# Two sequences in one tile, a second array shape and another load order in a pooled-attention and gated-convolution kernel

## The chip, the cores and the metric

The kernel runs on one core of one Trainium2 chip. The metric is the device time of one execution in microseconds (us), inputs and output in the chip's main memory. A core has five engines that run their own instruction streams: TensorE (PE in the profile, with weight loads as PEld), VectorE (DVE), ScalarE (ACT), GpSimd (POOL) and SyncE (SP). Here GpSimd does almost nothing but issue loads, and SP nothing but issue DMAs. The timed runs of the kernel before took 256.58, 256.73 and 257.45 us.

## The reference

Eight sequences of 576 rows, 8 heads of 64. Keys and values are averaged over groups of 8 rows (72 remain), attention is computed against these, and its result goes through a feed-forward block with a convolution of three taps along the sequence, one weight per channel, whose sigmoid gates the hidden layer.

```python
k_p = k.reshape(B, H, Sp, pool, D).mean(axis=3)          # pool = 8, Sp = 72
v_p = v.reshape(B, H, Sp, pool, D).mean(axis=3)
scores = scale * np.matmul(q, k_p.transpose(0, 1, 3, 2))
scores = scores - np.max(scores, axis=-1, keepdims=True)
attn = np.exp(scores)
attn = attn / (np.sum(attn, axis=-1, keepdims=True) + 1e-09)
x = np.matmul(attn, v_p)                                 # then [B, S, 8 * 64]
h = np.maximum(x @ w_in, 0.0)                            # w_in [512, 1024]
conv_out = sum of conv_w[k] * h shifted by k - 1 rows    # per channel
gate = 1.0 / (1.0 + np.exp(-conv_out))
out = (h * gate) @ w_out                                 # w_out [1024, 512]
```

## The kernel before

All matrix work is in bf16. The 576 rows of a sequence are ordered so that row 9p + c lies in column block c (9 blocks of 64). An attention tile is 128 rows by 8 heads: a sequence has four full tiles and one half tile. `groups = [[0], [1], [2, 3], [4, 5], [6, 7]]` (line 272) says which sequences share one: in a pair the two half tiles become one full tile, so a pair has 9 tiles, while sequences 0 and 1 have 5 each. The second sequence of a pair keeps its rows in another block order, and its convolution (`conv_runs`, line 683) is cut in 20 matmuls a block of channels in place of 16.

The steps of a sequence b are:

- `prep_k` (438) pools k by a matmul with the matrix pm, `prep_q` (484) transposes q on TensorE, `prep_v` (458, 462) adds v up on VectorE and spreads it into vm. The copies out of PSUM (449, 492) go to VectorE or ScalarE.
- Per tile: scores (517), the negative maximum (530), its addition (by TensorE, 550, in groups 0 and 1; by VectorE into sd, 542, later), the exponential into e (563), the transpose of e into eT (on TensorE with a copy, 575 and 589, or a DMA transpose issued by SP, 584, from group 3 on), values (600), division (613, 615) into x, and the transpose of x into xT (632 and 640 on TensorE, or a DMA transpose by SP, 624, for groups whose first sequence is 2 or more).
- The feed-forward part: w_in (645; for sequence 0 tile by tile, 666), the rectifier into hT (654, 676), a copy hX of hT with its two halves of 64 channels swapped (711), the convolution in four 64x64 quadrants (731), tanh (743), the gate and the product into gT (753, 754), w_out (761), the copy to osb (772), the store (783).

A step of the swap (`ffn_swap`, 711) is a copy by VectorE or ScalarE for sequences 0 to 3, and a DMA issued by SP for 4 to 7 (`SWAP_DVE = 4`). A swap serves two blocks of channels, so a sequence has four pairs of swaps.

The order of everything is the work of a planner, the class `Graph`. Each step is added with a key, an assumed duration on each engine that may do it, what must come before and which buffers it uses. `order` (91) keeps an assumed clock for each engine and takes the startable step of the smallest key; a step that two engines may do goes to the one with the smaller key or less work so far. The keys are sums of a slot per sequence and numbers of a table (`ATT`, `PREP_K`, `NUDGE` and so on). The result is one fixed program per engine. Each engine works through its own in order, and waits only for semaphores. Where TensorE has nothing to do early on, the planner puts in matmuls on a blank tile (432), which compute nothing that is used.

Loads go by GpSimd's queue (329 for q and k, 343 and 346 for v, 354 for w_in, 357 for w_out), with a cast from float32 to bf16; stores, transposes and swaps go by SP's queue.

Of the kernel before, what the change touches and what calls it, by code (L numbers as in the profile page):

```python
# [32 lines left out]
class Graph:  # L33
# [57 lines left out]
    def order(self):  # L91
# [5 lines left out]
        wire, mode, now, done = 0.0, None, 0.0, []  # L97
# [3 lines left out]
        spares = list(self.spares)  # L101
# [54 lines left out]

        while avail:
# [4 lines left out]
            for o in avail:  # L162
# [80 lines left out]
def kernel(  # L243
# [261 lines left out]
    def rows_of(g, t):  # L505
        return parts(g, t)[-1][1]
# [598 lines left out]
```

## Time and profile before

| | us |
|---|---|
| timed runs, median (lowest to highest) | 256.73 (256.58 to 257.45) |
| profiled execution, whole | 257.26 |
| profiled execution, span from first to last instruction | 255.2 |
| first full-speed slices of TensorE's clock | from about 24 |
| swaps on VectorE / ScalarE / by DMA | 14 / 18 / 32 instructions |

The profile has busy times per engine, groups of equal instructions (xcount, busy us, mean ns, idle time before them and what ended it), the chain of work that ended last, followed backwards from the end, timelines, and stretches of time with the busy time of each engine in them. Instructions that follow each other on an engine can overlap by some tens of nanoseconds, so that group times add up to a little more than the engine's. The table below is of groups and issues that the change touches.

```profile
L449 ACT CAST kT<-psum 64x288 bf16<-64x288 f32 x11 | 4.3, 393 | 2.4 <-PE psum L438 2.3
L589 DVE COPY eT<-psum 128x640 bf16<-128x640 bf16 x6 | 2.9, 485 | 1.5 <-PE psum L575 1.4
...
out_dram<-osb SPq DMA_DIRECT2D x72, 128.0 KB, 2.4
hX<-hT SPq DMA_DIRECT2D x32, 144.0 KB, 2.4
xT<-x SPq DMA_TRANSPOSE x27, 3.2
eT<-e SPq DMA_TRANSPOSE x18, 2.6
```

The last four rows are DMA issues: count, size, median time from issue to landing.

### The profile page before, as it was taken

What the parts mean: (1) busy time and instruction counts of PE and PEld (TensorE: products, weight loads), DVE (VectorE), ACT (ScalarE), POOL (GpSimd) and SP (SyncE); (2) the same over time, 40 slices, a digit from 0 to 9 for tenths busy, and PEclk for the clock granted to TensorE, in tenths of its full rate; (3) what the DMA queues carried; (4) which work ended last, traced back from release to release, by engine and by line L of the source; (5) the groups of instructions that cost most, each with busy time, mean ns of one, the idle gap of its engine ahead of it and who ended that gap; (6) DMA issues with size and microseconds to landing.
All of it is one profiled execution on the core that took longest, in us unless ns stands there. A gap on an engine that the chain in (4) does not pass through costs nothing.

```text
span 255.2 us, 7524 instructions
## 1 busy us (share of the span) xinstructions
PE 228.6 (90%) x3169; PEld 158.1 (62%) x3169; DVE 168.8 (66%) x363; ACT 164.8 (65%) x259; POOL 30.0 (12%) x50
## 2 busy tenths in 40 slices
PE   5758999989998899999999969879899889999992
PEld 1526888877776567567765536656565466676440
DVE  6557687799999998999568779411679711716200
ACT  2225547679899949986896455436688435758431
POOL 7753311302040004000001000000000000000000
PEclk9658999999999999999999999999999999999998
DMA  5999999999979558976408776668856859736356
GB/s 82 149 197 207 208 208 206 206 207 208 171 104 180 119 97 153 174 153 124 84 3 137 159 111 133 134 89 192 184 124 136 132 119 214 154 89 142 84 135 153
DMA packets 50682, 37.40 MB, mean 147 GB/s; under 512 B 29121, under 2 KB 43481, under 8 KB 50649
## 3 DMA queue, kind: packets, MB, share of 16 engines
q1 hardware_dynamic: 35176, 20.67, 40.7%
q0 software_dynamic: 15472, 16.26, 39.5%
q8 instruction: 24, 0.39, 0.6%
q14 instruction: 10, 0.07, 0.1%
HBM read 32.52 MB, written 9.44 MB: 164 GB/s over the span
## 4 chain that ended last, share of the span: by engine, by line
PE 49%; DVE 17%; DMA 14%; ACT 9%; SPq 4%; issue 3%; POOL 2%; ACTq 0%; POOLq 0%; DVEq 0%
PE psum L761 17%; PE psum L645 10%; PE psum L731 7%; DMA hX<-hT 6%; DMA qp<-in_q_dram 3%; DMA eT<-e 3%; DVE negm L530 3%; DVE x L615 3%; PE psum L666 3%; PE psum L600 3%; ACT hX L711 2%; PE psum L484 2%; PE psum L517 2%; ACT hT L654 2%; ACT e L563 2%
## 5 line engine op out<-in xcount | busy, mean ns | idle before, releaser
L761 PE MATMUL psum<-w_out_sb,gT 128*128 128x512 bf16 (+1 forms) x296 | 70.6, 379 | 0.7 <-DVE x L615 0.3
L645 PE MATMUL psum<-xT,w_in_sb 128*128 128x288 bf16 x448 | 59.2, 286 | 1.2 <-ACT xT L640 0.6
L645 PEld LDWEIGHTS <-w_in_sb 128*128 128x128 bf16 x448 | 42.5, 98 | 13.1 <-issue 0.8
L654 ACT ACTIVATE hT<-psum 128x576 bf16<-128x576 f32 x56 | 34.4, 649 | 18.1 <-PE psum L645 18.0
L743 ACT ACTIVATE tg<-psum 128x576 bf16<-128x576 f32 x64 | 38.0, 654 | 11.4 <-PE psum L731 6.7
L761 PEld LDWEIGHTS <-gT 128*128 128x128 bf16 (+1 forms) x296 | 27.1, 98 | 28.1 <-issue 1.0
L772 ACT COPY osb<-psum 128x512 f32<-128x512 f32 (+1 forms) x31 | 18.0, 583 | 24.4 <-PE psum L761 23.8
L731 PE MATMUL psum<-hX,dw 64*64 64x288 bf16 (+4 forms) x560 | 31.6, 249 | 2.4 <-DMA hX<-hT 2.4
L731 PEld LDWEIGHTS <-dw 64*64 64x64 bf16 x1120 | 25.4, 107 | 13.1 <-issue 11.6
L731 PE MATMUL psum<-hT,dw 64*64 64x288 bf16 (+4 forms) x560 | 31.8, 249 | 1.5 <-DVE x L615 0.5
L753 DVE TENSOR_SCALAR tg<-tg 128x576 bf16<-128x576 bf16 x64 | 19.7, 308 | 19.0 <-ACT tg L743 18.9
L530 DVE TENSOR_REDUCE negm<-psum 128x8 f32<-128x576 f32 (+2 forms) x37 | 26.9, 751 | 7.4 <-PE psum L517 7.0
L754 DVE TENSOR_TENSOR gT<-tg,hT 128x576 bf16<-128x576 bf16 x64 | 29.3, 458 | 2.2
L615 DVE TENSOR_TENSOR x<-psum,r 128x512 bf16<-128x512 f32 (+1 forms) x37 | 25.6, 691 | 1.5 <-DVE r L613 0.2
L600 PE MATMUL psum<-vm,eT 128*128 128x130 bf16 (+5 forms) x240 | 18.5, 222 | 7.0 <-DMA eT<-e 5.3
L613 DVE RECIPROCAL r<-psum 128x8 f32<-128x8 f32 (+1 forms) x37 | 7.4, 201 | 24.7 <-PE psum L600 24.5
L600 PEld LDWEIGHTS <-eT 128*128 128x128 bf16 (+1 forms) x240 | 14.2, 100 | 13.7 <-DMA eT<-e 8.3
L563 ACT ACTIVATE e<-sd 128x576 bf16<-128x576 f32 x27 | 18.0, 681 | 5.6 <-DVE sd L542 5.4
L711 ACT COPY hX<-hT 64x1152 bf16<-64x1152 bf16 x18 | 20.7, 1150 | 0.4
L542 DVE TENSOR_TENSOR sd<-psum,negm 128x576 f32<-128x576 f32 x27 | 19.6, 751 | 0.3
L438 PE MATMUL psum<-pm,kp 128*64 128x144 bf16 x288 | 13.6, 235 | 3.3 <-DMA kp<-in_k_dram 3.3
L492 ACT COPY qT<-psum 128x1152 bf16<-128x1152 bf16 (+2 forms) x13 | 12.2, 992 | 6.5 <-PE psum L484 6.5
(61 smaller groups left out, 221.0 us busy)
## 6 DMA issues: line engine op xcount, KB each, us to landing
out_dram<-osb SPq DMA_DIRECT2D x72, 128.0 KB, 2.4
hX<-hT SPq DMA_DIRECT2D x32, 144.0 KB, 2.4
v<-in_v_dram POOLq DMA_DIRECT2D x8, 512.0 KB, 9.9
kp<-in_k_dram POOLq DMA_DIRECT2D x7, 576.0 KB, 18.7
qp<-in_q_dram POOLq DMA_DIRECT2D x7, 576.0 KB, 12.9
w_in_sb<-in_moe_w_in_dram POOLq DMA_DIRECT2D x4, 256.0 KB, 9.5
w_out_sb<-in_moe_w_out_dram POOLq DMA_DIRECT2D x1, 1024.0 KB, 17.1
kp<-in_k_dram POOLq DMA_DIRECT2D x2, 288.0 KB, 5.3
```

The source lines that it names most:

```text
L530: nc.vector.tensor_reduce(out=a["m"][0:rows], in_=a["s"][0:rows, :, 0:2 * KW].rearrange("p a (h s) -> p a h s", s=Sp), axis=AX.X, op=OP.ma ...
L563: nc.scalar.activation(out=e[0:rows, 0:4 * KW].rearrange("p (a x) -> p a x", a=2), in_=a["d"][0:rows].rearrange("p a h s -> p a (h s)") if ...
L600: nc.tensor.matmul(out=a["o"][lo:hi, h // 4, (h % 4) * (D + 1):(h % 4 + x1 - x0) * (D + 1)], lhsT=a["eT"][:, j, lo:hi], rhs=buf("vm", b)[: ...
L615: nc.vector.tensor_tensor(out=a["x"][0:rows].rearrange("p (a h d) -> p a h d", a=2, d=D), in0=ov[:, :, :, 0:D], in1=r[0:rows].unsqueeze(3) ...
L645: nc.tensor.matmul(out=banks(ps)[:, j, 0:SC], lhsT=w_in_sb[dc][:, fb * P:(fb + 1) * P], rhs=buf("xT", g)[:, dc, i * S + j * SC:i * S + (j ...
L654: nc.scalar.activation(out=buf("hT", b)[:, fb, :].rearrange("p (a s) -> p a s", a=2), in_=banks(ps)[:, :, 0:SC], func=ACT.Relu, scale=0.5,)
L711: copy(out=buf("hX", b, f2)[r * D:(r + 1) * D, :, :], in_=buf("hT", b)[(1 - r) * D:(2 - r) * D, 2 * f2:2 * f2 + 2, :],)
L731: nc.tensor.matmul(out=cps[c * D:(c + 1) * D, r, lo:hi], lhsT=dw[r * D:(r + 1) * D, int(r != c), tap * n_fb + fb, :], rhs=hT[r * D:(r + 1) ...
L743: nc.scalar.activation(out=tg.rearrange("p (a s) -> p a s", a=2), in_=banks(ps)[:, :, 0:SC], func=ACT.Tanh, scale=0.5,)
L753: nc.vector.tensor_scalar(out=tg, in0=tg, scalar1=1.0, scalar2=None, op0=OP.add)
L754: nc.vector.tensor_tensor(out=buf("gT", g)[:, fb, i * S:(i + 1) * S], in0=tg, in1=buf("hT", b)[:, fb, :], op=OP.mult)
L761: nc.tensor.matmul(out=bank(ps)[0:rows, :], lhsT=buf("gT", g)[:, fb, t * P:t * P + rows], rhs=w_out_sb[:, fb, :], start=(fb == 0), stop=(f ...
```

## The change

The diff does several things at once.

1. `groups` becomes `[[0, 1], [2, 3], [4, 5], [6, 7]]`: sequences 0 and 1 share their half tiles. There are 36 attention tiles in place of 37, and sequence 1 takes the second block order. As groups are renumbered, `SHIFT_DVE` and `TURN_DMA` go down by one and mean the same pairs.
2. `X_DMA` 2 to 4: the pair [2, 3] now transposes x on TensorE with a copy, not by DMA.
3. `SWAP_DVE` 4 to 8: all swaps are copies by VectorE or ScalarE.
4. `prep_k`, `prep_q` and the scores get a second form in 64x64 quadrants (with half as many rows per matmul and twice or four times as many matmuls), and the planner chooses by the shape that the array is in (`form`).
5. The early loads get keys of their own, and w_in comes in two halves of its columns, not in four blocks of its rows.
6. The last output tile is copied in two halves of columns, by VectorE and ScalarE, and its two stores are issued by SP and by ScalarE.
7. Rings of buffers change in length, and the planner's assumed durations, its keys and its model of loads change.

```diff
-    X_DMA = 2
-    SHIFT_DVE = 2
-    TURN_DMA = 3
-    SWAP_DVE = 4
+    X_DMA = 4
+    SHIFT_DVE = 1
+    TURN_DMA = 2
+    SWAP_DVE = 8
...
-        ('a', 0): 4.21, ('a', 1): 2.02, ('a', 2): -82.33, ('a', 3): -9.19, ('a', 4): 6.54, ('a', 5): -14.37,
+        ('a', 0): -37.24, ('a', 1): 86.29, ('a', 2): -5.89, ('a', 3): -182.14, ('a', 4): -71.88, ('a', 5): -38.08,
...
+        def form(o, s):
+
+            choice = [(o.mode, o.engines["PE"], o.count)] if o.forms is None else o.forms
+            if o.like is not None:
+                choice = [c for c in choice if c[0] == o.like.mode]
+            best = None
+            for m, d, c in choice:
+                d = d if full else 2 * d
+                t = max(s, fetched(c, d))
+                late = t + d
+                if m != mode:
+                    late += self.SWITCH + self.LEAVE.get(mode, 0.0) + self.LEAVE.get(m, 0.0)
+                if best is None or late < best[0]:
+                    best = late, t, d
+                    o.mode, o.count = m, c
+            return best[1:]
...
-    groups = [[0], [1], [2, 3], [4, 5], [6, 7]]
+    groups = [[0, 1], [2, 3], [4, 5], [6, 7]]
...
-    rings = {"e": 4, "eT": 3, "negm": 3, "x": 5, "tg": 5, "osb": 5,
-             "hT": 2, "gT": 2, "xT": 2, "qT": 4, "kp": 4, "qp": 2, "hX": 4, "v": 2, "vm": 3, "kT": 4, "sd": 2, "r": 3, "s": 2}
+    rings = {"e": 6, "eT": 3, "negm": 3, "x": 4, "tg": 5, "osb": 5,
+             "hT": 2, "gT": 2, "xT": 2, "qT": 3, "kp": 3, "qp": 2, "hX": 3, "v": 2, "vm": 5, "kT": 5, "sd": 3, "r": 3, "s": 2}
...
-    w_in_sb = [const.tile([P, d_ff], BF16, name=f"w_in_sb{c}") for c in range(n_dmc)]
+    w_in_sb = [const.tile([P, n_dmc, d_ff // 2], BF16, name=f"w_in_sb{j}") for j in range(2)]
...
+                for f in range(2):
+                    rows = slice(f * TB, (f + 1) * TB)
+                    nc.tensor.matmul(
+                        out=banks(ps)[hh * D:(hh + 1) * D, f, half * Sp:(half + 1) * Sp],
+                        lhsT=k_rows[rows],
+                        rhs=pm[rows, c, f * Sp:(f + 1) * Sp],
+                        start=(c == 0),
+                        stop=(c == C - 1),
+                    )
...
+        if mode == QUARTER:
+            halves = [(lo + x, lo, b) for lo, hi, b in parts(g, t) for x in range(0, hi - lo, D)]
+            for n in range(4):
+                a, f = n // 2, n % 2
+                for lo, lo0, b in halves:
+                    for r in range(2):
+                        rows = slice(r * D, (r + 1) * D)
+                        c = t % 5 * P + lo - lo0
+                        nc.tensor.matmul(
+                            out=sp[lo:lo + D, r, n * Sp:(n + 1) * Sp],
+                            lhsT=buf("qT", b)[rows, f, a, c:c + D],
+                            rhs=buf("kT", b)[rows, 2 * f + a, r * Sp:(r + 1) * Sp],
+                            start=(n == 0),
+                            stop=(n == 3 and shift_by_dve(g, t)),
+                            skip_group_check=True,
+                        )
...
+    early = ["k0", "k0+", "q0", "pm", "v0", "ident", "q0+", "w0", "w1", "mask", "k1", "q1", "v1", "out",
+             "k2", "q2", "v2", "k3", "q3"]
+
+    def first(name):
+        return START - 40 + early.index(name) + nudge("l", name)
...
-            o = add(either(0.69, 0.585), key, None, after=[o], uses=[osb, sm])
+            if b == B - 1 and n == len(n_outs[b]) - 1:
+                o = [add(d, key, lambda t=t, sm=sm, x=x, copy=copy: ffn_copy(g, t, sm, copy, slice(x * P * 2, (x + 1) * P * 2)),
+                         after=[o], uses=[osb, sm])
+                     for x, (d, copy) in enumerate(((dve(0.4), nc.vector.tensor_copy), (act(0.4), nc.scalar.copy)))]
+                for x, (e, queue) in enumerate((("SP", nc.sync), ("ACT", nc.scalar))):
+                    add({e: 0.59}, key, lambda t=t, x=x, queue=queue: ffn_store(g, t, queue, x), after=o, uses=[osb], land=(2.0, 0, 1))
+                continue
+            o = add(either(0.69, 0.585), key, None, after=[o], uses=[osb, sm])
```

Where instructions stand is decided by the planner, so three places are shown as the two programs have them. The first is GpSimd's program at the start, before the change: kp and qp are loads of k and q, the first of each for sequence 0, and 128x4x256 is the part of q for its first tiles.

```order
L329 DMA kp_79<-in_k_dram 128x2x576 x2
L369 ISA
L369 AFFINE_SELECT pm<-pm 64x9x72 x2
L329 DMA qp_77<-in_q_dram 128x4x256
masks.py:197 MEMSET ident 128x128
masks.py:199 AFFINE_SELECT ident<-ident 128x128
L343 DMA v_91<-in_v_dram 128x4x512
L346 DMA v_91<-in_v_dram 64x512
L329 DMA qp_77<-in_q_dram 128x4x320
L388 MEMSET mask 128x15
L390 AFFINE_SELECT mask<-mask 128x15 x2
L354 DMA w_in_sb_68<-in_moe_w_in_dram 128x1024
```

The same place after it, from the identity matrix on:

```order
masks.py:199 AFFINE_SELECT ident<-ident 128x128
L354 DMA qp_75<-in_q_dram 128x4x256
L368 DMA v_88<-in_v_dram 128x4x512
L371 DMA v_88<-in_v_dram 64x512
L399 AFFINE_SELECT pm<-pm 64x9x72 x2
L354 DMA kp_78<-in_k_dram 128x4x576
L354 DMA qp_75<-in_q_dram 128x4x320
L354 DMA qp_76<-in_q_dram 128x4x576
L379 DMA w_in_sb_69<-in_moe_w_in_dram 128x4x512
L379 DMA w_in_sb_68<-in_moe_w_in_dram 128x4x512
L387 DMA w_out_sb<-in_moe_w_out_dram 128x8x512
```

The k of sequence 1 (kp_78) now stands ahead of the second part of q of sequence 0, its q right behind, and w_in after both; pm is built later.

The second place is SP's program where sequences 4 and 5 begin their convolutions, before the change:

```order
L624 DMA_TRANSPOSE xT_114<-x_106 128x4x128
L783 DMA out_dram<-osb_126 64x512 x2
L783 DMA out_dram<-osb_127 64x512 x2
L711 DMA hX_130<-hT_116 64x1152 x2
L624 DMA_TRANSPOSE xT_114<-x_107 128x4x128
L711 DMA hX_131<-hT_116 64x1152 x2
L711 DMA hX_132<-hT_116 64x1152 x2
L711 DMA hX_133<-hT_116 64x1152 x2
L711 DMA hX_130<-hT_117 64x1152 x2
```

And after it, where the last transposes of the pair [4, 5] (into xT_114) and the first of [6, 7] (into xT_115) stand:

```order
L696 DMA_TRANSPOSE xT_114<-x_107 128x4x128
L856 DMA out_dram<-osb_128 64x512 x2
L856 DMA out_dram<-osb_129 64x512 x2
L696 DMA_TRANSPOSE xT_115<-x_108 128x4x128
L856 DMA out_dram<-osb_125 64x512 x2
L856 DMA out_dram<-osb_126 64x512 x2
L696 DMA_TRANSPOSE xT_115<-x_109 128x4x128
```

All 32 swaps are gone from SP's program; transposes and stores remain.

The third place is VectorE's program in the same sequences, before the change (tg and gT are the gate and its product):

```order
L613 RECIPROCAL r_112<-psum 128x8
L615 TENSOR_TENSOR x_107<-psum,r_112 128x512
L753 TENSOR_SCALAR tg_120<-tg_120 128x576
L754 TENSOR_TENSOR gT_124<-tg_120,hT_116 128x576
L753 TENSOR_SCALAR tg_121<-tg_121 128x576
L754 TENSOR_TENSOR gT_124<-tg_121,hT_116 128x576
```

And after it:

```order
L783 COPY hX_131<-hT_116 64x1152
L685 RECIPROCAL r_111<-psum 128x8
L687 TENSOR_TENSOR x_110<-psum,r_111 128x512
L783 COPY hX_132<-hT_116 64x1152
L825 TENSOR_SCALAR tg_120<-tg_120 128x576
L826 TENSOR_TENSOR gT_123<-tg_120,hT_116 128x576
L685 RECIPROCAL r_112<-psum 128x8
L687 TENSOR_TENSOR x_107<-psum,r_112 128x512
L825 TENSOR_SCALAR tg_121<-tg_121 128x576
L826 TENSOR_TENSOR gT_123<-tg_121,hT_116 128x576
L783 COPY hX_130<-hT_116 64x1152 x2
```

The swaps stand among divisions and products in VectorE's own program; of all 64, VectorE now has 41 and ScalarE 23.

More of the change, by code (lines that the diff above doesn't have):

```diff
@@ L33 @@
 class Graph:
-    PIPE = {"PE": 0.22, "DVE": 0.14, "ACT": 0.14, "POOL": 0.10, "SP": 0.0}
+    PIPE = {"PE": 0.24, "DVE": 0.14, "ACT": 0.14, "POOL": 0.10, "SP": 0.0}
     SWITCH = 0.12
-    LEAVE = {(64, 64): 0.08}
-    STAY = 18.41
-    LAZY = 0.87
+    LEAVE = {(64, 64): 0.13}
+    STAY = 111.55
+    LAZY = 1.11
     BLOCK, PRELUDE, FETCH, FETCH_LOADING = 256, 66, 3.4, 6.2
@@ L96, in order @@
         banks = [None] * self.BANKS
-        wire, mode, now, done = 0.0, None, 0.0, []
+        wire, mode, now, done = 2.6, None, 0.0, []
         spent = {e: 0.0 for e in self.PIPE}
@@ L169, in order @@
                     if e == "PE":
-                        d = d if full else 2 * d
-                        s = max(s, fetched(o.count, d))
+                        s, d = form(o, s)
+                    if e == "POOL" and o.land is not None and len(landings) + o.dmas > self.IN_FLIGHT:
+                        s = max(s, landings[len(landings) + o.dmas - 1 - self.IN_FLIGHT])
                     k = o.key - (self.STAY if e == "PE" and o.mode == mode else 0)
@@ L483, in prep_q, with copy_q @@
             for hh in range(2):
-                nc.tensor.transpose(
-                    out=qps[hh * D:(hh + 1) * D, :, c - c0, :],
-                    in_=buf("qp", b)[:, 2 * half + hh, c * D:(c + 1) * D],
-                    identity=ident,
-                )
-    def copy_q(b, half, part, ps, copy):
+                q_rows = buf("qp", b)[:, 2 * half + hh, c * D:(c + 1) * D]
+                if mode == HALF:
+                    nc.tensor.transpose(out=qps[hh * D:(hh + 1) * D, :, c - c0, :], in_=q_rows, identity=ident)
+                    continue
+                for f in range(2):
+                    rows = slice(f * TB, (f + 1) * TB)
+                    nc.tensor.transpose(
+                        out=qps[hh * D:(hh + 1) * D, f, c - c0, :], in_=q_rows[rows], identity=ident[rows, rows]
+                    )
+    def copy_q(b, half, part, ps, mode, copy):
         c0, c1 = q_parts(b)[part]
@@ L493, in copy_q @@
             out=buf("qT", b)[:, :, half, c0 * TB:c1 * TB].rearrange("p f (c t) -> p f c t", t=TB),
-            in_=q_banks(b, part, ps)[:, :, 0:c1 - c0],
+            in_=q_banks(b, ps, mode)[:, :, 0:c1 - c0],
         )
@@ L661, in ffn_in_tile @@
     def ffn_in_tile(b, t, j, ps):
-        g, rows = where[b][0], rows_of(where[b][0], t)
+        g, rows = where[b][0], TB if t == 4 else P
         hps = banks(ps).rearrange("p a (f t) -> p a f t", t=P)
@@ L674, in ffn_relu_tile @@
     def ffn_relu_tile(b, t, ps):
-        rows = rows_of(where[b][0], t)
+        rows = TB if t == 4 else P
         nc.scalar.activation(
@@ L767, in ffn_out, with ffn_copy, ffn_store @@
             )
-    def ffn_copy(g, t, ps, copy):
+    def ffn_copy(g, t, ps, copy, columns=slice(0, d_model)):
         rows = rows_of(g, t)
         osb = buf("osb", g, t)
-        copy(out=osb[0:rows], in_=bank(ps)[0:rows, :])
-    def ffn_store(g, t):
+        copy(out=osb[0:rows, columns], in_=bank(ps)[0:rows, columns])
+    def ffn_store(g, t, queue, only=None):
         osb = buf("osb", g, t)
@@ L782, in ffn_store @@
         for j, (b, c) in enumerate(blocks):
-            nc.sync.dma_start(
-                out=out[b].rearrange("(p c) d -> c p d", c=C)[c],
-                in_=osb[j * TB:(j + 1) * TB, :],
-            )
+            if only in (None, j):
+                queue.dma_start(
+                    out=out[b].rearrange("(p c) d -> c p d", c=C)[c],
+                    in_=osb[j * TB:(j + 1) * TB, :],
+                )
     def pe(*columns):
@@ L952, in add_att @@
         lim = token("s")
-        o = add(pe(*[144] * 4 if not split else [170] * 4), key, lambda: att_scores(g, t, s),
+        o = add(pe(*[144] * 4 if not split else [170] * 4), key, None,
                 after=prepared(g, t), uses=[s, lim, e] + [x[b] for b in seqs for x in (qTt, ktok)], mode=mode, count=8 + 8 * split)
+        o.emit = lambda o=o: att_scores(g, t, s, o.mode)
+        o.forms = [(mode, o.engines["PE"], o.count), (QUARTER, 0.19, 32) if rows == P else (QUARTER, 0.17, 16)]
         o = add(dve(0.75), key, lambda: att_max(g, t), after=[o], uses=[ng, s])
```

193 lines of the change are left out of this document (107 added, 86 removed), and 18 rows, old and new, of the table NUDGE.

## The prediction

> **What bounds the kernel now.** I read the page first, then the moments at which the work of each pair of sequences is finished, then the engines' busy time between those moments. The page says which engine is fullest.
>
> ```profile
> span 255.2 us, 7524 instructions
> PE 228.6 (90%) x3169; PEld 158.1 (62%) x3169; DVE 168.8 (66%) x363; ACT 164.8 (65%) x259; POOL 30.0 (12%) x50
> ```
>
> An average of 90% says little: the stages differ. The last step of a sequence on VectorE is the product that fills gT (line 754), eight per sequence, so its 16th, 32nd, 48th and 64th instance mark the end of each pair. The timeline of VectorE has them here (start, duration, engine, line):
>
> ```profile
> 92.10 0.46 DVE L754 TENSOR_TENSOR gT<-tg,hT 128x576 bf16<-128x576 bf16 x1
> 135.65 0.46 DVE L754 TENSOR_TENSOR gT<-tg,hT 128x576 bf16<-128x576 bf16 x1
> 196.68 0.46 DVE L754 TENSOR_TENSOR gT<-tg,hT 128x576 bf16<-128x576 bf16 x1
> 238.15 0.46 DVE L754 TENSOR_TENSOR gT<-tg,hT 128x576 bf16<-128x576 bf16 x1
> ```
>
> The view of stretches, cut at these ends, then gives five stages, and cut finer inside the first, a second table (length, then busy PE, PEld, DVE, ACT, POOL, granted clock, DMA share, GB/s).
>
> ```profile
> 0.00:92.56 92.56, 80.28 (x1301) 61.70 (x1302) 75.68 (x162) 62.43 (x97) 26.63 (x45) 0.93 1.07 174
> 92.56:136.11 43.55, 43.10 (x604) 29.65 (x603) 36.65 (x79) 37.37 (x56) 3.36 (x5) 1.00 0.60 111
> 136.11:197.14 61.03, 54.24 (x698) 35.67 (x697) 37.84 (x78) 36.26 (x57) 0.00 (x0) 1.00 0.72 141
> 197.14:238.61 41.47, 39.04 (x517) 25.87 (x515) 18.65 (x46) 24.09 (x43) 0.00 (x0) 1.00 0.66 133
> 238.61:255.20 16.59, 11.99 (x56) 5.23 (x54) 0.00 (x0) 4.61 (x8) 0.00 (x0) 0.95 0.62 142
> ...
> 8.00:16.00 8.00, 4.83 (x50) 3.34 (x52) 6.50 (x13) 1.62 (x4) 4.90 (x10) 0.50 1.10 160
> 16.00:24.00 8.00, 7.55 (x67) 5.18 (x66) 3.72 (x7) 5.16 (x8) 3.74 (x6) 0.66 1.16 207
> ...
> 50.00:75.00 25.00, 23.43 (x468) 19.25 (x463) 24.20 (x52) 21.94 (x37) 4.29 (x6) 1.00 1.13 173
> 75.00:100.00 25.00, 23.17 (x294) 15.97 (x292) 24.45 (x49) 21.16 (x29) 2.04 (x4) 1.00 0.75 133
> ```
>
> Stage 1 is a slow start and then VectorE: from 50 to 100 us VectorE is busy 48.65 of 50 us (97.3%), and its 16.9 idle us (92.56 - 75.68) lie almost all in the head. Stage 2 is TensorE, 43.10 of 43.55. Stages 3 and 4 are neither: TensorE loses time while VectorE and ScalarE stand idle. The chain of waits and the issuing timeline of SP say why (start, us, what):
>
> ```profile
> 173.65 2.53 DMA hX<-hT
> 177.57 2.47 DMA hX<-hT
> 180.18 3.77 DMA hX<-hT
> 213.61 2.50 DMA hX<-hT
> 217.47 3.83 DMA hX<-hT
> ...
> 170.47 2.50 SPq L783 DMA_DIRECT2D out_dram<-osb  x4
> 173.01 1.24 SPq L711 DMA_DIRECT2D hX<-hT  x2
> 174.35 1.25 SPq L624 DMA_TRANSPOSE xT<-x  x1
> 175.69 8.33 SPq L711 DMA_DIRECT2D hX<-hT  x11
> ```
>
> SP issues back to back from 170 to 184 us. Each swap costs it 0.62 us (1.24 / 2), each transpose 1.25, and the convolutions of sequences 4 and 5 stand behind three swaps in a row: 2.53 + 2.47 + 3.77 = 8.77 us of the chain.
>
> **The change, stage by stage.** Counts are taken from the order of the instructions up to the same marks; durations are means of these groups (xcount, then busy us, mean ns), and for TensorE pieces of the chain and, for the convolutions alone, a stretch with the two of them (40 matmuls).
>
> ```profile
> L615 DVE TENSOR_TENSOR x<-psum,r 128x512 bf16<-128x512 f32 (+1 forms) x37 | 25.6, 691 | 1.5 <-DVE r L613 0.2
> L613 DVE RECIPROCAL r<-psum 128x8 f32<-128x8 f32 (+1 forms) x37 | 7.4, 201 | 24.7 <-PE psum L600 24.5
> L530 DVE TENSOR_REDUCE negm<-psum 128x8 f32<-128x576 f32 (+2 forms) x37 | 26.9, 751 | 7.4 <-PE psum L517 7.0
> L542 DVE TENSOR_TENSOR sd<-psum,negm 128x576 f32<-128x576 f32 x27 | 19.6, 751 | 0.3
> L711 DVE COPY hX<-hT 64x1152 bf16<-64x1152 bf16 x14 | 6.7, 481 | 4.3 <-ACT hT L654 4.0
> L711 ACT COPY hX<-hT 64x1152 bf16<-64x1152 bf16 x18 | 20.7, 1150 | 0.4
> L462 DVE TENSOR_TENSOR vm<-v,mask 128x960 bf16<-128x960 bf16 x8 | 9.2, 1154 | 0.1
> ...
> 20.63 0.76 DVE L530 TENSOR_REDUCE negm<-psum 128x8 bf16<-128x576 f32 x1 [3.99 <-PE psum L517]
> ...
> 236.65 13.96 PE psum L761 x64
> 198.47 0.94 PE psum L600 x18
> 43.68 0.68 PE psum L438 x18
> 46.33 1.00 PE psum L484 x36
> 39.27 0.61 PE psum L517 x8
> ...
> 230.70:231.75 1.05, 0.95 (x40) 0.76 (x40) 1.00 0.72 167
> ```
>
> *Stage 1 (to the 16th product).* Less of the next sequences' attention now stands ahead of the mark. On VectorE: 3 maxima, 2 shifts and 7 divisions fewer (3 x 0.751 + 2 x 0.751 + 7 x 0.892 = 10.0 us), one vm product and three v additions fewer (1.15 and, at half of that each, 1.7), four swaps and four eT copies more (eight at the swap's 0.481, 3.8), and small copies and clears that I put at 2.3 fewer, four or five at a swap's price: -11.3 us. Instructions that follow each other overlap a little: the busy times of all its groups sum to 180.0 us, the engine's own is 168.8, so I scale by 0.94: 75.7 - 10.6 = 65.1. The idle time was 16.9. The 3.99 us wait before the third maximum is filled now, because tiles 0 and 1 run to the end before the second part of q is wanted; against that, that part is issued behind the whole k of sequence 1 (0.59 MB as it lands in bf16; at the 207 GB/s of the rows above an estimated 2.9 us later). I take 14 us, bounds 11 to 18. **65.1 + 14 = 79.1 us**, 13.5 earlier than before. That is work deferred, not saved.
>
> *Stage 2.* It comes back here: 5 maxima and 5 shifts more (7.5), 6 divisions (5.4), 4 swaps (1.9), three v additions and two vm products (4.0), three xT copies that DMA transposes made before (1.4 at a swap's price), one output copy fewer: together about +20.0, x 0.94 = 18.8, so VectorE has 36.65 + 18.8 = 55.4 us. TensorE, by the pieces above (line 761: 0.218 each, 600: 0.052, 438: 0.038, 484: 0.028, 517: 0.076), gets 42 value matmuls, 54 of k, 54 of q, 15 scores' worth and 61 transposes (as values) more and 8 output projections less: 2.2 + 2.1 + 1.5 + 1.1 + 3.2 - 1.7 = 8.4, so 51.5 busy. The bound moves to VectorE. At the 97.3% that it reaches where it is the bound: **57.0 us**; the mark falls at 136.1, as before (136.1).
>
> *Stage 3.* TensorE loses work that came earlier: 28 output projections, the time of 54 q transposes and 24 scores, 6.1 + 1.5 + 1.8 = 9.4. With every wait kept it would last 61.03 - 9.4 = 51.6. The swaps leave SP: VectorE makes 10 of these 16, ScalarE 6, at 0.481 and 1.150 us against 2.5 to 3.8 in a queue. VectorE stays near 36 us (4 maxima, 4 shifts fewer), so it has room. If every wait went, TensorE's busy time would remain, 54.24 - 9.4 = 44.8; the 8.77 us of the chain are enough for that. I take the middle, because eT and xT transposes still wait in SP's queue: **48.2 us**, bounds 44.8 and 51.6.
>
> *Stage 4.* TensorE has 8.1 us more (32 output projections at 0.218, 16 scores at 0.076), so 49.6 with waits kept. Here I keep them all: the two hX waits (2.50 + 3.83) go, but VectorE takes 7.7 us and ScalarE 10 us more, 7 swaps at 1.150 among them. **49.6 us**, bounds 47.1 (busy, 39.04 + 8.1) and 49.6.
>
> *The end.* Four output projections fewer (0.9 us). The last two stores go out by two queues, which saves one issue: 0.62 by the nearest row, and the last copy is cut in two halves that run side by side, at most 0.3 more. **15.1 us.**
>
> Sum: 79.1 + 57.0 + 48.2 + 49.6 + 15.1 = 249.0 us against this execution's span of 255.2, so -6.2 us. The profiled execution took 257.26 in all; the median of the three timed runs is 256.73, which makes the forecast 250.5 us.
>
> **Small unknowns.** The 64x64 form of k, q and scores was never run here for these. It is used for 7 of the 32 k and q preparations and 3 of the 36 tiles. At half of the present piece, by columns, it saves 6 x 0.34 + 1 x 0.25 + 3 x 0.15 = 2.7 us; at the 0.024 us that a convolution matmul takes (0.95 / 40), 36 of them cost 0.86 against 0.68, so it loses up to 1.5. I take 0, as in the sums, nearest to the preparations' own rows. The exponential that writes in another order (3 times) lies between its present mean and twice that, off the bound. w_in in halves moves the same bytes; both halves are asked for later, and TensorE has sequence 1's preparations to do until then.
>
> **Rivals.** (a) *VectorE does not hold 97% in stage 2.* In the present stage 2 it ran at 36.65 / 43.55 = 84%, waiting for the others' chains. At that rate 55.4 us take 66.0, which is 9.0 more: 259.5. It turns the sign below 88%, where the 6.2 us are used up. For it: the swaps queue behind maxima and divisions on an in-order engine. Against it: the same mixture ran at 97% from 50 to 100 us. (b) *The transposes, not the swaps, hold the second half.* Stage 3 keeps its 51.6: 253.9. For it: SP issues them at 1.25 us each and they are all still there after the mark. (c) *All waits on swaps go*, in stages 3 and 4: 3.4 and 2.5 less at most, 244.6 to 247. (d) *The gain of (c) is spent by (a) in part*: within 0.3% of now. (e) *The clock stays low.* The rows from 8 to 24 us show 0.50 and 0.66 granted; if 0.50 lasted until 24, the 7.55 busy us there become 7.55 x 0.66 / 0.50 = 10.0, which gives 252.9.
>
> The Trainium skill, "TensorE: Matmul & The Clock Gate", section "What's actually happening", says that the array starts at half clock and is released after a busy window of about 3.4 us; the rows of 0.50 and 0.66 agree, and by that rule (e) comes if the shorter chains of the new head leave such windows half empty.
>
> (f) *The loads' issues are held up by more copies on VectorE.* The longest issue of a v load, beside the mean of all eight:
>
> ```profile
> 58.87 0.96 POOL L343 DMA_DIRECT2D v<-in_v_dram  x1 [7.69 <-DVE vm L462]
> ...
> L343 POOL DMA_DIRECT2D v<-in_v_dram x8 | 6.2, 780 | 48.0 <-DVE vm L462 33.2 <-DVE tg L753 12.5 <-DMA qp<-in_q_dram 2.3
> ```
>
> It is 0.18 us above the mean, and the loads run ahead of their use after the head; were twenty issues held so and none of it hidden, 3.6 us would be lost: 254.1.
>
> The Trainium skill, "SBUF — State Buffer", section "SBUF: two separate sides", says that a VectorE copy in a two-port mode locks GpSimd out of writing descriptors; it speaks against 27 more such copies, and the row above fits it, at 0.2 us a time.
>
> **How the numbers follow.** Forecast (247 to 253): 0.52. (a): 0.15. (b): 0.13. (c): 0.08. (d): 0.08. (e): 0.02. (f): 0.02. About 0.3% is what a measurement can tell from no change here, 256.0 to 257.5. Faster is the forecast with (b), (c), (e), (f): 0.77; same (d): 0.08; slower (a): 0.15. The range takes in (b), most of (a) and the upper part of (c): 244.5 to 258.5.
>
> **What would show it.** Right: the 16th product near 79, the 32nd near 136, VectorE above 95% in between; no DMA hX in the chain; the 48th near 183. Wrong: the 32nd product past 142 (a), or the chain in stage 3 full of eT and xT transfers (b). A first product earlier than 79 with the rest unchanged would mean that the head was worth more than I allow.

## The result, and the profile after

| | before | after |
|---|---|---|
| timed runs, median (lowest to highest), us | 256.65 (254.4 to 257.45) | 244.87 (243.7 to 245.72) |
| profiled execution, whole, us | 257.26 | 245.72 |
| its span, us | 255.2 | 244.0 |

The ratio of the two is 0.9551, with a 95% interval of 0.9479 to 0.9623: 11.8 us faster by the medians, where 6.2 were forecast (250.5).

The page of the changed kernel has this at its head (busy us, share of the span, instructions):

```profile
span 244.0 us, 7852 instructions
PE 220.9 (91%) x3354; PEld 154.3 (63%) x3377; DVE 182.0 (75%) x398; ACT 168.3 (69%) x264; POOL 29.1 (12%) x48
```

TensorE is busy 7.7 us less than before (228.6), VectorE 13.2 more (168.8). The five stages are cut as in the prediction, at the ends of the 16th, 32nd, 48th and 64th product into gT, which stands on line 826 now. The timeline of VectorE (start, duration) and the view of stretches (length, then busy PE, PEld, DVE, ACT, POOL, granted clock, DMA share, GB/s):

```profile
79.56 0.46 DVE L826 TENSOR_TENSOR gT<-tg,hT 128x576 bf16<-128x576 bf16 x1
136.34 0.46 DVE L826 TENSOR_TENSOR gT<-tg,hT 128x576 bf16<-128x576 bf16 x1
183.63 0.46 DVE L826 TENSOR_TENSOR gT<-tg,hT 128x576 bf16<-128x576 bf16 x1
227.45 0.46 DVE L826 TENSOR_TENSOR gT<-tg,hT 128x576 bf16<-128x576 bf16 x1
```

```profile
0.00:80.02 80.02, 68.71 (x1357) 52.21 (x1361) 65.00 (x146) 52.15 (x82) 24.39 (x41) 1.00 1.05 173
80.02:136.80 56.78, 55.33 (x813) 39.62 (x816) 54.78 (x114) 46.12 (x74) 4.71 (x7) 1.00 0.69 122
136.80:184.09 47.29, 43.57 (x611) 29.75 (x615) 35.40 (x79) 33.73 (x53) 0.00 (x0) 1.00 0.53 92
184.09:227.91 43.82, 42.30 (x531) 27.97 (x537) 25.70 (x61) 33.01 (x51) 0.00 (x0) 1.00 0.47 98
227.91:244.00 16.09, 11.01 (x51) 4.80 (x49) 1.12 (x2) 3.30 (x6) 0.00 (x0) 0.94 0.54 131
```

| stage | before | predicted | after |
|---|---|---|---|
| 1 | 92.56 | 79.1 | 80.02 |
| 2 | 43.55 | 57.0 | 56.78 |
| 3 | 61.03 | 48.2 | 47.29 |
| 4 | 41.47 | 49.6 | 43.82 |
| end | 16.59 | 15.1 | 16.09 |

The second mark stands where it stood (136.80 against 136.11). All of the gain comes behind it: 119.1 us before, 107.2 now. In that part TensorE is busy 96.9 us in place of 105.3, and idle 10.3 in place of 13.8. Of the 8.4 us, an estimated 5 are work that is no longer there, done ahead of the mark or not at all. By the weight loads behind the mark there are 9 output projections, 20 scores and 72 transposes of q fewer, and 36 small transposes in place of the last, which took 0.48 us: at the prediction's prices 9 x 0.218 + 20 x 0.076 + 72 x 0.028 - 0.48 = 5.0. The rest is matmuls that waits no longer stretch (stage 4, below) and some records that the trace lacks. So work makes somewhat less than half of the gain, and waits the rest.

The view of waits of TensorE, in stage 3 (us in total, times, longest), before and then after, shows what is left:

```profile
PE psum L600 <- DMA eT<-e: 3.6, 4, 1.7
PE psum L731 <- DMA hX<-hT: 1.6, 3, 0.8
```

```profile
PE psum L672 <- DMA eT<-e: 2.2, 1, 2.2
PE psum L717 <- DMA xT<-x: 1.3, 1, 1.3
```

No wait on hX is left, but one on eT and one on xT, the transposes by DMA that SP issues.

### The profile page after: what moved, and what is told of

It is laid out like the page before. It is cut to its first block, busy times and chain, and to the rows that moved or that the text cites. A ratio compares the mean times of both kernels' runs of the same rounds, so it can differ in the third digit from the quotient of the medians.

```text
span 244.0 us, 7852 instructions
## 1 busy us (share of the span) xinstructions
PE 220.9 (91%) x3354; PEld 154.3 (63%) x3377; DVE 182.0 (75%) x398; ACT 168.3 (69%) x264; POOL 29.1 (12%) x48
## 4 chain that ended last, share of the span: by engine, by line
PE 51%; DVE 26%; ACT 8%; DMA 7%; issue 5%; POOL 0%; SPq 0%; DVEq 0%; ACTq 0%; POOLq 0%
PE psum L833 16%; PE psum L717 14%; PE psum L803 7%; DVE negm L598 5%; DVE gT L826 4%; PE psum L672 3%; DVE sd L610 3%; DMA kp<-in_k_dram 3%; PE psum L738 3%; DVE tg L825 2%; ACT hT L726 2%; DVE hX L783 2%; DVE x L687 2%; DVE v L503 2%; DMA eT<-e 2%
## 5 line engine op out<-in xcount | busy, mean ns | idle before, releaser
L833 PE MATMUL psum<-w_out_sb,gT 128*128 128x512 bf16 x266 | 66.6, 379 | 2.0 <-issue 0.8
L717 PE MATMUL psum<-xT,w_in_sb 128*128 128x288 bf16 x448 | 61.1, 286 | 2.0 <-DMA xT<-x 1.3
L833 PEld LDWEIGHTS <-gT 128*128 128x128 bf16 x288 | 26.0, 98 | 25.9 <-issue 0.7
L783 DVE COPY hX<-hT 64x1152 bf16<-64x1152 bf16 x41 | 18.7, 458 | 18.3 <-ACT hT L726 15.4
L803 PE MATMUL psum<-hT,dw 64*64 64x224 bf16 (+3 forms) x576 | 30.9, 246 | 0.8 <-ACT tg L815 0.7
L803 PE MATMUL psum<-hX,dw 64*64 64x288 bf16 (+3 forms) x576 | 30.7, 246 | 0.0
L598 DVE TENSOR_REDUCE negm<-psum 128x8 f32<-128x576 f32 (+1 forms) x36 | 25.9, 750 | 2.4 <-PE psum L585 2.2
L783 ACT COPY hX<-hT 64x1152 bf16<-64x1152 bf16 x23 | 26.4, 1150 | 0.5
L687 DVE TENSOR_TENSOR x<-psum,r 128x512 bf16<-128x512 f32 x36 | 24.9, 692 | 1.2
L672 PE MATMUL psum<-vm,eT 128*128 128x130 bf16 (+5 forms) x240 | 18.5, 222 | 4.2 <-DMA eT<-e 2.2
L685 DVE RECIPROCAL r<-psum 128x8 f32<-128x8 f32 x36 | 7.3, 201 | 8.8 <-PE psum L672 8.7
```

What stands on the lines that cost most here:

```text
L598: nc.vector.tensor_reduce(out=a["m"][0:rows], in_=a["s"][0:rows, :, 0:2 * KW].rearrange("p a (h s) -> p a h s", s=Sp), axis=AX.X, op=OP.ma ...
L672: nc.tensor.matmul(out=a["o"][lo:hi, h // 4, (h % 4) * (D + 1):(h % 4 + x1 - x0) * (D + 1)], lhsT=a["eT"][:, j, lo:hi], rhs=buf("vm", b)[: ...
L687: nc.vector.tensor_tensor(out=a["x"][0:rows].rearrange("p (a h d) -> p a h d", a=2, d=D), in0=ov[:, :, :, 0:D], in1=r[0:rows].unsqueeze(3) ...
L717: nc.tensor.matmul(out=banks(ps)[:, j, 0:SC], lhsT=w_in_block(dc, fb), rhs=buf("xT", g)[:, dc, i * S + j * SC:i * S + (j + 1) * SC], start ...
L783: copy(out=buf("hX", b, f2)[r * D:(r + 1) * D, :, :], in_=buf("hT", b)[(1 - r) * D:(2 - r) * D, 2 * f2:2 * f2 + 2, :],)
L803: nc.tensor.matmul(out=cps[c * D:(c + 1) * D, r, lo:hi], lhsT=dw[r * D:(r + 1) * D, int(r != c), tap * n_fb + fb, :], rhs=hT[r * D:(r + 1) ...
```

## The experiments

Three theories were set against each other. Theory 1: the gain is that SP's queue is relieved in the second half. Theory 2: it is the new order, that is the table. Theory 3: it is the head, by the clock, and the array's shape. Each ratio below is against the kernel before on the same chip, with its interval; the changed kernel itself stands at 0.9551 (0.9479 to 0.9623).

### The swaps as DMAs again

```diff
-                        b, fb // 2, r, nc.sync.dma_start if o.engine == "SP" else copier(o))
+                        b, fb // 2, r, nc.sync.dma_start if b >= 4 else copier(o))
```

> The changed kernel with one part undone: the swaps of sequences 4 to 7 are DMAs issued by SP again, at the places where their copies stand, and everything else keeps its order. Theory 1 (the gain is in the second half, by SP's queue): the third stage gets back some of the 8.77 us of hX waits and the fourth some of its 6.33, so 6 to 10 us more than the changed kernel's 244.9, that is 251 to 255. Theory 2 (the gain is the new order and keys, which place work so that a late swap harms nobody): within 1.5 us, 244 to 246.5. Theory 3 (the gain is the head: the clock and the shape of the array): the same as theory 2 here, with all five marks where they are.

265.41 us, ratio 1.0317 (1.0232 to 1.0402): 8% slower than the changed kernel, twice what theory 1 expected and more than the whole change brought. Stages 1 and 2 are as they were. Stages 3 and 4 of this kernel, the waits of TensorE in them, and one stretch of SP's issues (start, us, what):

```profile
136.76:192.75 55.99, 46.53 (x615) 30.94 (x615) 31.27 (x69) 27.96 (x47) 0.00 (x0) 1.00 0.60 119
192.75:246.37 53.62, 47.01 (x538) 29.88 (x536) 21.86 (x51) 25.73 (x44) 0.00 (x0) 0.94 0.57 124
```

```profile
PE psum L803 <- DMA hX<-hT: 13.3, 14, 4.5
PE psum L672 <- DMA eT<-e: 2.2, 1, 2.2
```

```profile
172.14 7.09 SPq L783 DMA_DIRECT2D hX<-hT  x5
```

TensorE now waits fourteen times for swaps, 13.3 us, where the kernel before has five such waits in these two stages, 2.4 us; and the stages grow by 18.5. The new order leaves no slack for a swap that takes 2.4 us of flight behind a queue.

### The swaps as copies in the kernel before

```diff
-                        b, fb // 2, r, nc.sync.dma_start if o.engine == "SP" else copier(o))
+                        b, fb // 2, r, nc.vector.tensor_copy if b >= 4 else copier(o))
```

> The kernel before with one part of the change alone: the swaps of sequences 4 to 7 are VectorE copies at the places where the DMAs stood, order otherwise kept. Theory 1: the hX waits (8.77 us in the third stage, 6.33 in the fourth) go and 32 copies of 0.48 us lie in VectorE's free time there, so 5 to 9 us less than before: 248 to 252, with the third stage at 53 to 56 in place of 61.0. Theory 2 or 3: less than 2 us gained, since eT and xT transfers stand next in SP's queue: 255 to 257.

254.3 us, ratio 0.9879 (0.9805 to 0.9953): 3 us, between the two. Its stages 3 and 4, its waits in stage 3, and the end of a piece of its chain of waits:

```profile
135.32:195.92 60.60, 53.36 (x698) 34.98 (x697) 45.18 (x94) 36.27 (x58) 0.00 (x0) 1.00 0.57 105
195.92:235.63 39.71, 38.40 (x517) 25.61 (x515) 25.73 (x62) 24.09 (x43) 0.00 (x0) 1.00 0.40 80
```

```profile
PE psum L600 <- DMA eT<-e: 4.6, 5, 1.7
```

```profile
183.84 0.45 DVE hX L711
...
184.33 0.32 DVE tg L753
184.67 0.46 DVE gT L754
```

Stage 3 hardly moved (61.03 to 60.60): the hX waits are gone, the waits on eT grew from 3.6 to 4.6 us, and at its end the copies, the gates and the products follow each other on VectorE without a gap, since the copies stand as late in its program as the DMAs did. A wait was removed and the next one stood behind it.

### The transposes of x for sequences 2 and 3 by DMA again

```diff
     def att_turn_out(g, t, ps):
+        if g == 1:
+            return
...
     def att_copy_out(g, t, copy):
+        if g == 1:
+            return att_out(g, t)
```

> The changed kernel with one part undone: x of sequences 2 and 3 is transposed by DMAs issued by SP, at the place of the copies, in place of 36 TensorE transposes and 9 copies; order otherwise kept. If the part costs what its rows say and nothing hides it, undoing it saves up to 2 us of TensorE and 3 to 4 us of copies in the second stage, where VectorE is the bound: 241 to 243.5. If the nine DMA transposes at 1.25 us of issue and some 3 us of flight are waited for by w_in of sequences 2 and 3, it costs 2 to 6 us: 247 to 251. By theory 1 (only the swaps matter) it stays within 1 us of 244.9.

256.55 us, ratio 0.9953 (0.9917 to 0.999): nearly all of the gain is gone, and more than the 2 to 6 us of the second expectation. It is lost in one stage. Stage 2 of this kernel, SP's issues in it, and one piece of its chain:

```profile
78.97:149.05 70.08, 58.54 (x787) 40.60 (x786) 54.30 (x111) 43.18 (x69) 4.70 (x7) 0.90 0.68 116
```

```profile
91.31 8.22 SPq L696 DMA_TRANSPOSE xT<-x  x4
99.62 2.53 SPq L860 DMA_DIRECT2D out_dram<-osb  x2
102.26 1.27 SPq L656 DMA_TRANSPOSE eT<-e  x1
```

```profile
104.94 7.43 DMA eT<-e
```

And one row of VectorE's timeline:

```profile
97.62 0.69 DVE L687 TENSOR_TENSOR x<-psum,r 128x512 bf16<-128x512 f32 x1 [6.07 <-DMA xT<-x]
```

VectorE has the same work as in the changed kernel (54.30 us against 54.78) and does it in 70.08 us in place of 56.78. The transposes of x go out ahead of those of e in the same queue while loads are still running, and one eT is 7.43 us from its issue to its landing. There are also only four buffers for x, and each is held until its transpose has landed: the row shows VectorE standing 6.07 us until it can write the next x. TensorE waits 6.1 us behind that and 5.1 on the eT, 11.2 of the 13.3 us that the stage grows by.

### One shape of the array

```diff
-            o.emit = lambda o=o, half=half, t=t: prep_k(b, half, t, o.mode)
+            o.emit = lambda o=o, half=half, t=t: prep_k(b, half, t, HALF)
...
-        o.emit = lambda o=o: att_scores(g, t, s, o.mode)
+        o.emit = lambda o=o: att_scores(g, t, s, mode)
```

The copies of k and the two steps of q are set to HALF likewise.

> The changed kernel with one part undone: every preparation of k and q and every tile's scores in the old array shape, order kept. As predicted (the second form is worth nothing): within 0.7 us of 244.9. If the shorter pieces count (36 small matmuls in 0.41 us against 0.7, seven times, and three tiles' scores) and lie where TensorE is the bound: 1 to 2.5 us more, 246 to 247.5. By theory 3, in which the array's shape is a large part of the gain: 3 us or more, 248 and above.

247.42 us, ratio 0.9586 (0.9518 to 0.9654), whose interval holds that of the changed kernel for the most part. Its first two stages:

```profile
0.00:79.42 79.42, 70.14 (x1229) 53.64 (x1230) 64.87 (x146) 52.28 (x82) 24.36 (x41) 1.00 1.04 172
79.42:136.18 56.76, 56.07 (x815) 39.80 (x814) 54.76 (x114) 46.27 (x74) 4.70 (x7) 1.00 0.72 123
```

TensorE has 1.4 us more to do in stage 1, and the first two marks come no later. So the six of the seven small preparations that lie there save TensorE time where it isn't wanted. (One of them took 0.48 to 0.51 us; the 0.41 of the expectation is what the planner assumes.) Stage 3, with the seventh in it, took 49.14 us, 1.85 longer, but at a granted clock of 0.97. By the times alone 3 us are not excluded: the ratios are 0.9 us apart, and each interval reaches some 1.8 us to either side. The marks speak against it.

### The clock at the head

In the kernel before, six blank matmuls were put where TensorE stood; in the changed kernel, all twelve that the planner had put in were left out. They compute nothing that is used.

```diff
     def prep_q(b, half, part, ps):
+        if b == 0 and part == 1 and half == 0:
+            for _ in range(6):
+                fill(ps)
```

```diff
     def fill(ps):
-        nc.tensor.matmul(out=bank(ps), lhsT=blank[:, 0:P], rhs=blank, start=True, stop=True)
+        pass
```

> The kernel before with six matmuls on the blank tile added where TensorE stands from 12.8 to 15.9 us (before the second part of q of sequence 0); they compute nothing that is used. Theory 3 (the low clock from 8 to 24 us, granted 0.50 and 0.66, is a good part of the loss of the kernel before): the clock is 0.9 or more from 16 us on, up to 2.6 busy us of the slice from 16 to 24 are saved, and the first mark and the end come 2 us or more earlier: 253 to 255. Theories 1 and 2: the clock rises, but VectorE bounds what follows, and the end moves by less than 0.7 us: 256 to 257.5.

> The changed kernel without the twelve matmuls on the blank tile (they compute nothing that is used), order kept. Theory 3: the clock is granted later (0.5 to 0.7 from 8 to 24 us), and the five marks come 2 to 5 us later: 247 to 250. Theories 1 and 2: the head has room, the first mark moves by less than 1 us: 244 to 246.

The first: 256.39 us, ratio 0.9985 (0.9951 to 1.0018). The second: 245.67 us, ratio 0.9599 (0.9554 to 0.9643). From 16 to 24 us the stretch of the first reads:

```profile
16.00:24.00 8.00, 6.99 (x81) 4.53 (x75) 5.80 (x12) 5.92 (x10) 3.83 (x6) 1.00 1.17 207
```

There the clock is at 1.00 where it was 0.66, and the first mark falls at 90.41 in place of 92.56. But 1.75 of these 2.15 us are lost again in stage 4 (43.22 against 41.47), and the timed runs show no difference. In the second, TensorE's early matmuls are slower (ten transposes of e take 1.38 us, where five take 0.45 with the blanks), and the first mark moved by 0.5 us (80.55). Theory 3 falls with these as far as it is the clock.

### The old table with the new parts, and the new table with the old paths

The first has the table of the kernel before (from `PIPE` to `NUDGE`) in the changed kernel, with X_DMA, SHIFT_DVE, TURN_DMA and SWAP_DVE as changed. The second:

```diff
-    X_DMA = 4
+    X_DMA = 2
...
-    SWAP_DVE = 8
+    SWAP_DVE = 4
```

> The changed kernel with the planner's table of the kernel before (assumed durations, keys, nudges), all other parts of the change kept: pairs, copies for all swaps, x of 2 and 3 on TensorE, second form, w_in in halves, last store on two queues; the order is planned anew. Theory 1 (the parts make the gain): 245 to 250. Theory 2 (the parts are worth what the undone swaps showed in the kernel before, 3 us, and the rest is the table): 252 to 258, with waits in the second half again. After the first four runs the second is the likelier: undoing one part of the changed kernel costs up to 20 us, which is more than the change brought.

> The changed kernel with its new table, but SWAP_DVE = 4 and X_DMA = 2 as before, and the order planned anew for them. Theory 2 in its plain form (the new table is what gains): 245 to 250. If table and parts only gain together, as the run with the old table and the new parts says (22 us slower than before): 260 or more. By theory 1 (the paths alone): 256 to 260, what the two undone parts bring back less what the planner saves by a better order.

279.35 us, ratio 1.089 (1.0845 to 1.0935), and 267.89 us, ratio 1.04 (1.0346 to 1.0454). The new parts without the new table, and the new table without two of the parts, are both slower than the kernel before. The longest waits of TensorE are on eT in both: 10.3 us in eight waits in the first, 8.2 us in two in the second.

These two are planned anew, so more than the named part differs. The old table also has no keys for the early loads, and the first of the two reaches its first mark only at 122.80 us: its loss can't be put down to the second half alone.

### The stores off SP's queue

The 36 stores of sequences 2 to 5, two for each of 18 tiles, are issued by GpSimd, whose loads are nearly all issued by then. First in the changed kernel, then in the kernel before:

```diff
-            add({"SP": 1.18}, key, lambda t=t: ffn_store(g, t, nc.sync), after=[o], uses=[osb], land=(2.0, 0, 1))
+            add({"SP": 1.18}, key, lambda t=t: ffn_store(g, t, nc.gpsimd if g in (1, 2) else nc.sync), after=[o], uses=[osb], land=(2.0, 0, 1))
```

```diff
-            nc.sync.dma_start(
+            (nc.gpsimd if g in (2, 3) else nc.sync).dma_start(
```

> The changed kernel with the stores of sequences 2 to 5 issued by GpSimd, whose last load is issued at 127 us, in place of SP, order kept. If what is left of SP's queue costs the third stage its two waits on DMA transposes (2.2 and 1.3 us) and the fourth 0.4: 2 to 4 us less, 241 to 243. If these two waits are the flight of a transfer that starts late for another reason, or GpSimd's stores cost VectorE time: 244 to 247.

> The kernel before with the stores of sequences 2 to 5 issued by GpSimd in place of SP, order kept, swaps still DMAs. If SP's queue as a whole is what the third stage waits for (each store 0.6 us of issue, 36 of them, between the swaps and transposes): 3 to 6 us of that stage, 251 to 254. If only the swaps count, or the flight of the transfers and not their issue: less than 1.5 us, 255.5 to 257.

The changed kernel: 245.83 us, ratio 0.9549 (0.9504 to 0.9594), nothing. The two waits are as long as they were with these entries gone, so issue is not what they wait for:

```profile
PE psum L672 <- DMA eT<-e: 2.2, 3, 1.4
PE psum L717 <- DMA xT<-x: 1.3, 1, 1.3
```

The kernel before: 250.61 us, ratio 0.9738 (0.9697 to 0.978), 6.4 us from one line that moves no work between computing engines. Its stages 3 and 4:

```profile
134.92:191.36 56.44, 52.96 (x698) 35.36 (x697) 37.75 (x78) 36.04 (x57) 11.67 (x22) 1.00 0.79 153
191.36:230.94 39.58, 38.40 (x517) 25.78 (x515) 18.68 (x46) 24.20 (x43) 6.29 (x12) 1.00 0.67 140
```

4.6 us come from stage 3 and 1.9 from stage 4, with the same matmuls. So SP's queue did hold the second half of the kernel before. The flights got no shorter with the stores gone (medians from issue to landing: hX 2.4 us in both, eT 3.6 in place of 2.6, xT 3.9 in place of 3.2), so what was relieved is SP's issuing, not the transfers. The chain of waits of the kernel before has four of these issues in it, from 170.47 us on, ahead of the first swap. The last of them and that swap (start, us, what):

```profile
172.37 0.59 SPq L783
...
173.65 2.53 DMA hX<-hT
```

The Trainium skill, "DMA: Bandwidth & Descriptors", section "Rules for kernel authors", says that spreading DMAs over issuing engines only saves sequencer issue time; this run agrees, and here that time was worth 6.4 us.

### Both reliefs in the kernel before

Swaps as copies and stores by GpSimd, the two edits above together.

> The kernel before with both reliefs of SP's queue and nothing else of the change: swaps of sequences 4 to 7 as VectorE copies where the DMAs stood, stores of sequences 2 to 5 issued by GpSimd; order kept. If the two reliefs add up (3.0 and 6.4 us alone): 247 to 248.5, that is four fifths of the change without its table. If they relieve the same waits: 250 to 251.5, and what the change has beyond that (about 6 us) needs the new order. If the copies, late as they stand, make VectorE the bound of the third stage's end: 251 to 254.

251.59 us, ratio 0.9805 (0.9756 to 0.9855): no better than the stores alone. Stage 3:

```profile
135.24:193.30 58.06, 52.38 (x692) 35.10 (x697) 45.21 (x94) 36.29 (x57) 11.62 (x22) 1.00 0.60 109
```

That is 1.6 us longer than with the stores alone. The chain of waits has hX copies, gates and products on VectorE from 176 to 185 us again. Where the order is the old one, copies of the swaps by VectorE are worth nothing once the queue is short. Sharing them with ScalarE, as the change does, was not tried there.

### The last store on one queue

```diff
-                    add({e: 0.59}, key, lambda t=t, x=x, queue=queue: ffn_store(g, t, queue, x), after=o, uses=[osb], land=(2.0, 0, 1))
+                    add({e: 0.59}, key, lambda t=t, x=x, queue=queue: ffn_store(g, t, nc.sync, x), after=o, uses=[osb], land=(2.0, 0, 1))
```

> The changed kernel with the last two stores both issued by SP. If the second queue saves one issue (0.62 us) at the very end: 0.4 to 0.9 us more, 245.3 to 245.8, all of it in the last stage. If the store on ScalarE's queue starts or lands later than SP's would: no change or less.

246.69 us (243.76 to 246.88), ratio 0.959 (0.9532 to 0.9648), too wide for half a microsecond. In the profiles the end takes 16.54 us against 16.09, but six kernels with both queues show 15.97 to 16.38, so that one issue more can only be guessed at here. The end of the changed kernel shows why it isn't more (start, duration):

```profile
238.20 0.42 DVE L844 COPY osb<-psum 128x256 f32<-128x256 f32 x1 [10.29 <-PE psum L833]
239.06 0.69 DVE L844 COPY osb<-psum 128x512 f32<-128x512 f32 x1 [0.44 <-ACT osb L844]
...
238.66 0.37 ACT L844 COPY osb<-psum 128x256 f32<-128x256 f32 x1 [0.75 <-DVE osb L844]
```

The two halves run one after the other, not side by side (ScalarE's starts when VectorE's ends), and the tile that was split is the last but one in the order: a whole copy of 0.69 us follows, and both of its stores go out by SP.

## Why the prediction was right, and where it was not

**Stage 1: right.** VectorE's work came out at 65.00 us (predicted 65.1), the idle time at 15.0 (14). The reason holds: giving TensorE 1.4 us more, or slowing its early matmuls, leaves this mark within 0.6 us.

**Stage 2: right.** VectorE has 54.78 us (55.4) and is busy 96.5% of the stage (97.3%). Rival (a), a fall to 84%, did not come. But I had costed x on TensorE as a price of this stage and never as what allows it: by DMA the stage is 13.3 us longer. The sum was right because the change had the part in it; I could not have said what the part was for. Two readings of the sum need mending. Its terms give 19.5 and not 20.0 (20.2 less one output copy, 0.68 us on VectorE). And TensorE was put at 51.5 busy us and has 55.33, 97.4% of the stage: it did 72 output projections, 8 more than before, where I had 8 fewer. So "the bound moves to VectorE" is half the story. From 109 us to the mark the chain of waits is nearly all VectorE's, but the two engines are about equally full, and with one shape of the array the chain of this stage runs mostly on TensorE. That the 3.8 us that I had missed there did not move the mark was luck.

**Stage 3: right, and the reason half right.** Predicted 48.2, measured 47.29, with 43.57 busy (44.8). Half of the waits were to stay, and 3.5 us on eT and xT stayed. But the waits were not the ones I had priced: the 8.77 us of swap flights in the chain are not time in which TensorE stood still. Of its 6.8 idle us in this stage 1.6 were waits on swaps and 3.6 on eT. That SP's queue made the waits is shown by the stores. That copies take the waits away is shown only in the new order; in the old one eT waits and a late VectorE took their place. Rival (b) described just that, and is what happens to the kernel before when it gets the copies alone.

**Stage 4: the step that failed**, and the largest part of the miss: 49.6 predicted, 43.82 measured, 5.8 us, more than the 5.0 by which the five terms missed the span. It failed at its first half, "TensorE has 8.1 us more (32 output projections at 0.218, 16 scores at 0.076)". The groups of weight loads in this stage, before and after:

```profile
L761 PEld LDWEIGHTS <-gT 128*128 128x128 bf16 x59 | 5.1, 98 | 5.4
L517 PEld LDWEIGHTS <-qT 128*128 128x128 bf16 x4 | 0.3, 97 | 0.0
```

```profile
L833 PEld LDWEIGHTS <-gT 128*128 128x128 bf16 x81 | 7.5, 98 | 7.8 <-issue 0.2
L585 PEld LDWEIGHTS <-qT 128*128 128x128 bf16 x4 | 0.3, 98 | 0.2
```

It was 22 projections and no scores, 22 x 0.218 = 4.8 us. I had counted by places in the order, up to the matmuls that belong to a mark. The mark is on VectorE, and by the time of it TensorE stands elsewhere in its own program, so that projections counted into stage 4 were done in the stages before, most of them in stage 2. That is 3.4 us. The second half, "with waits kept", failed too: waits also stretch what counts as busy. The same matmuls took 39.04 us with the swaps' waits and 38.40 without them, in both the run with copies and the run with stores by GpSimd. 38.40 + 4.8 = 43.2, which is what two kernels with the changed order show in this stage, without blanks and with stores by GpSimd:

```profile
182.14:226.90 44.76, 43.07 (x538) 27.96 (x537) 25.77 (x60) 33.02 (x51) 0.00 (x0) 1.00 0.48 97
```

```profile
183.45:228.42 44.97, 43.22 (x538) 27.87 (x537) 25.78 (x60) 33.01 (x51) 9.57 (x18) 1.00 0.47 97
```

The changed kernel's own 42.30 lacks some records (531 matmuls against 538). The stage is TensorE's work plus 0.9 to 1.8 us in the kernels with the same work in it, which take 43.81 to 44.97.

**The end: 1.0 us too short.** TensorE's work fell by 0.98 (predicted 0.9), but the issue and the copy that I took off (0.62 and up to 0.3) were taken off another tile than the last.

**Small unknowns.** The 64x64 forms at 0: the run can't tell it from 0 (0.9586 against 0.9551), and where six of the seven preparations lie the marks don't move.

**Rivals.** The measured 244.87 lies outside the forecast's 247 to 253 and in (c)'s 244.6 to 247, which had a chance of 0.08. (c)'s condition came, since no wait on a swap is left, but its sum didn't: stage 3 keeps 3.5 us of waits on transposes, and stage 4 is short because TensorE's work in it is less than I had it. That the total fell into (c)'s range is luck. (e) did not come: the granted clock reads 1.00 at the head, and slower matmuls there cost 0.5 us of the first mark at most. Nor did (f): with 27 more copies on VectorE the eight issues of v loads take 760 ns in the mean, 780 before.

**What stays open.** Which of the table's numbers matter wasn't tried, nor the pairing of sequences 0 and 1 by itself. That order and parts need each other is shown; how much each would bring with a table made for it is not. No run reproduces the whole gain in the kernel before: the stores alone bring 6.4 of the 11.8 us, by a relief that the change itself does not make, and the change's own swaps bring 3 there. What the moved work brings by itself was not measured. Stage 3 took from 45.02 to 47.29 us in kernels with the same work in it, so some 2 us of it come and go without the work changing.

## What to carry to other kernels

Undoing one part of a change measures what the rest has come to need, not what the part brought: here single parts cost up to 20 us to undo in a change worth 12, and brought 3 when made alone. Before moving work off a queue, count what else that queue issues; taking other entries off it (here stores, on which no wait of TensorE shows) can be worth more than taking off the transfers that it waits for. The time of a transfer in the chain of waits is not the time that its engine stands still; the view of waits has that. When work is counted into stages by an order, count each engine to its own place at the mark.

## What the runs showed that I had not expected

The granted clock and the speed of the matmuls are not the same thing. Three rows of TensorE's timeline, all of the same 18 matmuls: the kernel before, after blanks; the changed kernel, after a gap of 3.63 us; and its first without blanks.

```profile
5.91 0.75 PE L438 MATMUL psum<-pm,kp 128*64 128x144 bf16 x18 [1.88 <-DMA kp<-in_k_dram]
```

```profile
8.86 1.29 PE L469 MATMUL psum<-pm,kp 128*64 128x144 bf16 x18 [3.63 <-DMA kp<-in_k_dram]
```

```profile
8.21 1.29 PE L469 MATMUL psum<-pm,kp 128*64 128x144 bf16 x18 [3.30 <-DVE pm L415]
```

0.75 us against 1.29, though the stretch from 8 to 16 us has a granted clock of 1.00 in both of the last two. The Trainium skill, "TensorE: Matmul & The Clock Gate", section "What's actually happening", has the array at half clock until a window of about 3.4 us was busy, and again after an idle one; the last two durations agree with it (3.60 us of blanks and then the gap in one, nothing but two small matmuls before it in the other), and the granted clock of these stretches does not. The first row agrees less well: its matmuls are at full speed after 2.74 us of blanks. So the head of the changed kernel is slow too, for some 5 us, and it does not matter, because the first mark hardly follows TensorE's early matmuls, as the run without blanks shows.
